# A three-stage kernel whose key and query loads, weight narrowing and dummy products are rearranged

## The chip, the cores and the metric

The program runs on one core of one Trainium2 chip. The metric is the device time of one launch, in microseconds (us). The kernel before was timed three times; each time also covers a little outside the profiled span.

## The reference

Three stages run one after the other. The first is a gated linear attention over 4 batches, 8 heads, 768 steps and head dimension 40, written as a recurrence over time:

```python
m_new = np.maximum(f_gate[:, :, t] + m, i_gate[:, :, t])
f_stab = np.exp(f_gate[:, :, t] + m - m_new)
i_stab = np.exp(i_gate[:, :, t] - m_new)
C = f_stab[:, :, None, None] * C + i_stab[:, :, None, None] * np.einsum('bhd,bhe->bhde', vt, kt)
n = f_stab[:, :, None] * n + i_stab[:, :, None] * kt
h_tilde = np.einsum('bhde,bhe->bhd', C, qt)
y[:, :, t] = sigmoid(o_gate[:, :, t]) * h_tilde / np.maximum(np.abs(np.einsum('bhd,bhd->bh', n, qt)[:, :, None]), 1.0)
```

The second is a soft mixture of experts over the 3072 tokens of width 320 (8 experts with 4 slots each, hidden width 1024, softmax over the tokens and over the slots). The third is an MLP, `relu(x @ w_in) ** 2 @ w_out`, with hidden width 2048.

## The kernel before

The 32 heads of all batches go in 11 groups of three (the last has two), and the 768 steps in 6 chunks of 128, so that the first stage is a loop over 66 units (group g, chunk c); unit i is 6g + c. The loop is software-pipelined: unit i issues the score products of unit i + 2 (`e_st`, L454), the decay exponentials of unit i + 3 (`e_exp`, L437, ScalarE), their mask (`e_sel`, L444, GpSimd), the product of both (`e_pm`, L466, VectorE), the state update (`e_u` L479, `e_uc` L498, `e_mask` L514), and for every second unit the products with v (`e_av`, L539), beside the product of q with the state (`e_inter`, L524). Between them a list of fillers is advanced: the gating of x, the expert logits of a batch that is done, and, as the last in rank, `win_all`.

`win_all` brings the weights w_in into a form that the third stage uses. They come in 10 windows of 128 x 1024 words (L163, 512 KB each) in two halves of the tile `stage`, and each window is narrowed to 128 x 512 by two ScalarE instructions (L140, L141) and two VectorE instructions (L143, L147). A filler stops at each `yield`; the letter says at which point of a unit it may go on ("W" once a unit, "A" for ScalarE, "n" for VectorE).

The program has its own order: no scheduler moves anything. All loads are issued by SyncE (SP) in the order of the program, and a request waits there until its buffer is free, with everything behind it. A group's k (three blocks of 40 x 768 words, 120 KB each, `load_kb`, L202) and q (120 x 768 words, 360 KB, `load_q`, L206) lie in one of two buffers, `par0` and `par1`, by the group's parity. The k of group g + 1 is requested at chunk 0 of group g, right before its q, and so into the buffer of group g - 1. Its k is last read by `e_st`, which runs two units ahead, and its q by `e_inter` of its last chunk. Other loads in the same queue are x (128 x 640, 320 KB, L221), v and k by tokens (369 and 360 KB, L215), the expert weights w1 (16 of 640 KB, L116) and w2 (16 of 640 KB, L123; the first two of them go into `stage` when `win_all` is done with it), and w_out (L962).

The start is a string, `START`, that is run token by token: `~30` stands for 30 dummy bf16 products on the identity matrix (`warm`, L192), `M2` for `e_mb` of chunk 2 (L423), `T0` for `e_st`, and `1f` and the like for steps of the gate preparation of chunks 0 and 1 (2: chunks 2 and 3; 3: chunks 4 and 5); `2q` are transposes (L331) and `2l` is a subtraction on VectorE (L351) that `M2` reads. After the 66 units come the rest of the experts (from 160 us on) and the third stage (from about 208 us on, L1283 to L1369).

Of the kernel before, what the change touches and what calls it, by code (L numbers as in the profile page):

```python
# [32 lines left out]
WO = (4, 5, 9)  # L33
START = "~30 1f 1i 1m 1h 1p 1b 1B 1aG 1r 2f 1u 1A 1v 1q 1l M0 2iG E0 M1 K0 W T0 T1 2m E1 K1 3f 2p 2b 2a ~14 2h 3i 3m 2B Z0 2r 2A 2v 2u P0 3p 3bG D0 3h Z1 ~3 2q 2l M2 E2 D0 P1 3a 3A 3B K2 D0 D0 3r 3u D0 | 3l 3v 3q | D1 D1 | D1 D1 D1 |"
REBIAS = 2.0**-112
# [7 lines left out]
def kernel(  # L43
# [16 lines left out]
    nc = tc.nc  # L60
# [73 lines left out]

    def narrow(dst, nt_, src, res=None):
        hi = src.rearrange("p (n w) -> p n w", w=2)[:, :, 1]
        low = src.bitcast(U16).rearrange("p (n w) -> p n w", w=4)[:, :, 1]
        di = dst.bitcast(I32)
        yield "A"
        nc.scalar.activation(dst, hi.bitcast(F32), AF.Copy, scale=REBIAS)  # L140
        nc.scalar.activation(nt_, low, AF.Copy, scale=2.0**-13, bias=2.0**-14 - 0.5)  # L141
        yield "n"
        nc.vector.scalar_tensor_tensor(  # L143
# [12 lines left out]
    def win_all():  # L156
# [13 lines left out]
        for n, (i, h) in enumerate(wins):  # L170
            yield "W"
            t2 = load(n + 1) if n + 1 < len(wins) else None
            yield from narrow(wi[:, i, NW * h : NW * h + NW], raw[:, 4 * NW : 5 * NW], t)
            t = t2
# [15 lines left out]
    def warm(n, t=None):  # L190
        for _ in range(n):
            nc.tensor.matmul(dum if t is None else t[:, 0:256], lhsT=zb[:, 0:128], rhs=zb, start=True, stop=True)  # L192

    kin, vin, xb = {}, {}, {}
    kbd = [par[i][0 : 3 * D, 0 : 3 * S].rearrange("p (j s) -> p j s", j=3) for i in range(2)]
# [8 lines left out]
    def load_q(g, cs=slice(0, S)):  # L204
        h0, nh = groups[g]
        nc.sync.dma_start(out=qin[g][0 : nh * D, cs], in_=q_t[h0 * D : (h0 + nh) * D, cs])  # L206

# [634 lines left out]
    def run(seq):  # L842
        for ch in seq.split():
            if ch[0] == "~":
                warm(int(ch[1:]))
            elif ch[0] in "MEKTP":
                {"M": e_mb, "E": e_exp, "K": e_sel, "T": e_st, "P": e_pm}[ch[0]](0, int(ch[1:]))
            elif ch[0] in "123":
                begin[ch[0]][ch[1]](*ch[2:])
            else:  # L850
                begin[ch[0]](*ch[1:])
# [10 lines left out]
    xq = [(b, c) for b in range(1, B) for c in range(0, NC, 2)]  # L862
    for i, (g, c) in enumerate(units):
        if c == 0 and g + 1 < NG:
            load_kb(g + 1)
            load_q(g + 1)
# [594 lines left out]
```

## Time and profile before

| | us |
|---|---|
| three runs | 410.29, 415.21, 408.58 |
| their median | 410.29 |
| the profiled execution, as timed | 411.04 |
| its span, from the first to the last instruction | 409.3 |
| mean granted clock of TensorE | 0.986 |
| TensorE (PE) busy | 383.4 |
| VectorE (DVE) busy | 263.7 |
| ScalarE (ACT) busy | 252.9 |
| GpSimd (POOL) busy | 101.5 |

All numbers of the rows below belong to the one profiled execution, whose time outside the span is 411.04 - 409.3 = 1.7 us. PEclk is the granted clock of TensorE as a share of 2.4 GHz; 0.50 is its lower level of 1.2 GHz. A matmul of fp32 data shows as two records.

### The profile page before, as it was taken

To read this page: it belongs to the slowest core of one execution; us is meant where nothing else is said; L and a number is where in the kernel's file an instruction comes from. 1 tells how busy PE (TensorE), PEld (TensorE's weight loads), DVE (VectorE), ACT (ScalarE), POOL (GpSimd) and SP (SyncE) were. 2 spreads that over 40 slices of the span, in tenths; PEclk is the share of its full clock that TensorE was granted. 3 is DMA by queue.
4 is the path that set the end of the run, shared out by engine and by line. 5 is a ranking of instruction groups with operands and counts; after the bars stand their busy time and mean duration, and the time that the engine had idled before them with its cause. 6 is when DMAs were issued, how large, how long until landed. Compare 5 with 4: busy or idle time off the path is not lost.

```text
span 409.3 us, 9150 instructions
## 1 busy us (share of the span) xinstructions
PE 383.4 (94%) x3435; PEld 337.0 (82%) x3435; DVE 263.7 (64%) x612; ACT 252.9 (62%) x575; POOL 101.5 (25%) x208
## 2 busy tenths in 40 slices
PE   6798987999699999999898999999999999999996
PEld 4697776888698887543377999999999999999996
DVE  8847787987457666545579965655655655655551
ACT  3678667657265654334479786667667667667662
POOL 5555555656654765500000000000000000000000
PEclk9799999999999999999999999999999999999999
DMA  7587569759975976879800001001001001001001
GB/s 200 169 319 245 197 208 348 217 160 346 281 246 186 285 218 254 262 260 360 339 1 2 0 16 50 2 0 66 2 1 66 1 2 64 2 0 66 2 2 64
DMA packets 18566, 56.37 MB, mean 138 GB/s; under 512 B 2346, under 2 KB 6154, under 8 KB 18138
## 3 DMA queue, kind: packets, MB, share of 16 engines
q1 hardware_dynamic: 18522, 55.79, 40.7%
q8 instruction: 27, 0.44, 0.4%
q14 instruction: 17, 0.14, 0.1%
HBM read 51.85 MB, written 3.93 MB: 136 GB/s over the span
## 4 chain that ended last, share of the span: by engine, by line
PE 69%; DMA 10%; DVE 6%; issue 4%; ACT 4%; POOL 4%; SPq 1%; DVEq 0%; POOLq 0%; ACTq 0%
PE ps_mb L1359 16%; PE ps_st L1359 15%; PE ps_lt L1359 8%; DMA par<-in_q_t_dram 7%; PE ps_st L454 6%; PE ps_o L1283 4%; DMA ring<-in_w_dram 3%; PE ps_o L539 3%; PE ps_o L524 3%; PE ps_st L479 2%; PE ps_m L1283 2%; PE ps_mb L423 2%; PE ps_m L654 1%; POOL cbd L514 1%; PE ps_st L1079 1%
## 5 line engine op out<-in xcount | busy, mean ns | idle before, releaser
L1306 DVE CAST hi<-ring 128x512 fp32r<-128x512 f32 x91 | 38.8, 426 | 60.8 <-ACT ring L1305 50.7
L437 ACT ACTIVATE w<-ps_mb,qt 128x128 f32<-128x128 f32 x192 | 56.6, 368 | 33.3 <-PE ps_mb L423 28.5
L1307 DVE TENSOR_TENSOR lo<-ring,hi 128x512 fp32r<-128x512 f32 x96 | 66.5, 692 | 10.0
L1288 ACT ACTIVATE ring<-ps_o 128x512 f32<-128x512 f32 x65 | 38.9, 599 | 36.6 <-PE ps_o L1283 36.6
L454 PE MATMUL ps_st<-par 120*128 120x128 f32 (+1 forms) x384 | 56.3, 284 | 3.9 <-DMA par<-in_q_t_dram 3.9
L1305 ACT ACTIVATE ring<-ring 128x512 f32<-128x512 f32 x91 | 57.5, 632 | 2.9
L454 PEld LDWEIGHTS ps_st<-par 120*128 120x128 f32 (+1 forms) x384 | 50.0, 198 | 4.9 <-issue 3.9
L1359 PE MATMUL ps_mb<-wohlh,hi 128*128 128x320 f32 x160 | 49.6, 311 | 0.0
L1359 PE MATMUL ps_mb<-wohlh,lo 128*128 128x320 f32 x160 | 49.5, 310 | 0.0
L1359 PE MATMUL ps_mb<-wohll,hi 128*128 128x320 f32 x160 | 49.3, 309 | 0.0
L1359 PE MATMUL ps_st<-wohlh,hi 128*128 128x320 f32 x144 | 44.8, 311 | 0.0
L1359 PE MATMUL ps_st<-wohlh,lo 128*128 128x320 f32 x144 | 44.7, 310 | 0.0
L1359 PE MATMUL ps_st<-wohll,hi 128*128 128x320 f32 x144 | 44.6, 310 | 0.0
L444 POOL TENSOR_SCALAR_AFFINE_SELECT w<-w 128x384 f32<-128x384 f32 (+1 forms) x66 | 35.2, 536 | 36.3 <-ACT w L437 33.1
L466 DVE TENSOR_TENSOR p<-ps_st,w 128x384 f32<-128x384 f32 (+1 forms) x66 | 35.5, 538 | 6.2 <-POOL w L444 3.8
L524 PE MATMUL ps_o<-cbd,par 120*128 120x123 f32 (+1 forms) x110 | 26.0, 318 | 7.9 <-POOL cbd L514 4.5
L1359 PEld LDWEIGHTS ps_mb<-wohll,hi 128*128 128x128 f32 x160 | 30.1, 188 | 1.3
L1288 ACT ACTIVATE ring<-ps_m 128x512 f32<-128x512 f32 x31 | 18.6, 599 | 18.8 <-PE ps_m L1283 18.8
L1359 PEld LDWEIGHTS ps_mb<-wohlh,hi 128*128 128x128 f32 x160 | 30.0, 188 | 0.0
L1359 PEld LDWEIGHTS ps_mb<-wohlh,lo 128*128 128x128 f32 x160 | 30.0, 188 | 0.0
L539 PE MATMUL ps_o<-par,p 128*64 128x41 f32 x768 | 29.1, 232 | 0.0
L1359 PEld LDWEIGHTS ps_st<-wohll,hi 128*128 128x128 f32 x144 | 27.1, 188 | 1.3
(267 smaller groups left out, 781.2 us busy)
## 6 DMA issues: line engine op xcount, KB each, us to landing
ring<-in_w_dram SPq DMA_DIRECT2D x24, 640.0 KB
stage<-in_w_in_dram SPq DMA_DIRECT2D x10, 512.0 KB
par<-in_w_dram SPq DMA_DIRECT2D x6, 640.0 KB
out_dram<-ring SPq DMA_DIRECT2D x24, 160.0 KB
par<-in_v_s_dram SPq DMA_DIRECT2D x10, 369.0 KB
par<-in_k_s_dram SPq DMA_DIRECT2D x10, 360.0 KB
par<-in_k_t_dram SPq DMA_DIRECT2D x29, 120.0 KB
par<-in_q_t_dram SPq DMA_DIRECT2D x9, 360.0 KB
```

What stands on the lines that cost most here:

```text
L437: nc.scalar.activation(w[:, j, :], mb[:, 128 * j : 128 * j + 128], AF.Exp, bias=qt3[:, c, h0 + j : h0 + j + 1])
L444: nc.gpsimd.affine_select(out=w, in_=w, pattern=[[0, nh], [1, 128]], compare_op=ALU.is_ge, fill=0.0, base=0, channel_multiplier=-1)
L454: nc.tensor.matmul(st[:, 128 * j : 128 * j + 128], lhsT=kbd[g % 2][0:nd, j, ts_], rhs=qin[g][0:nd, ts_], start=True, stop=True,)
L466: nc.vector.tensor_tensor(out=p, in0=sts.pop((g, c))[:, 0 : nh * 128].rearrange("p (n t) -> p n t", n=nh), in1=ws.pop((g, c)), op=ALU.mult,)
L524: nc.tensor.matmul(pos[g, c // 2][:, o0 : o0 + nv], lhsT=qin[g][0:nd, 128 * c : 128 * c + 128], rhs=cbds[g, c - 1][0:nd], start=True, stop ...
L539: nc.tensor.matmul(po[t0 : t0 + 64, o0 : o0 + DV], lhsT=p[:, j, t0 : t0 + 64], rhs=vin[g][:, c, j, :], start=True, stop=True,)
L1283: nc.tensor.matmul(t, lhsT=gst[n][:, 128 * k : 128 * k + 128], rhs=cst[tg], start=True, stop=True)
L1288: nc.scalar.activation(r, t, AF.Relu)
L1305: nc.scalar.activation(r, r, AF.Square)
L1306: nc.vector.tensor_copy(hi, r)
L1307: eng.tensor_tensor(out=lo, in0=r, in1=hi.bitcast(F32), op=ALU.subtract)
L1359: nc.tensor.matmul(acc[u][:, 0:DM], lhsT=l_[:, 128 * u : 128 * u + 128], rhs=wohl[r_, f // 8][:, f % 8, :], start=(f == 0 and a == 0), sto ...
```

## The change

Four things are changed at once. The two ScalarE instructions of a window are no longer issued one after the other: `narrow(..., apart=True)` stops after each of them until the next unit, so that a window takes at least three units and the ten windows stretch over more of the loop. `START` has 12 more dummy products in its first run of them and 10 more in its second, and a new kind, `~~5`, between `2q` and `M2`: 20 fp32 products, 10 of 128 columns and 10 of 41, each on 40 rows, alternately from row 0 and from row 64 and into two banks. The q of a group is requested as 128 rows; the last 8 belong to the next head and are not read. The k of group g + 2 is requested at chunk 4 of group g; that is two chunks before the place where it was requested (chunk 0 of group g + 1).

```diff
-START = "~30 1f 1i 1m 1h 1p 1b 1B 1aG 1r 2f 1u 1A 1v 1q 1l M0 2iG E0 M1 K0 W T0 T1 2m E1 K1 3f 2p 2b 2a ~14 2h 3i 3m 2B Z0 2r 2A 2v 2u P0 3p 3bG D0 3h Z1 ~3 2q 2l M2 E2 D0 P1 3a 3A 3B K2 D0 D0 3r 3u D0 | 3l 3v 3q | D1 D1 | D1 D1 D1 |"
+START = "~42 1f 1i 1m 1h 1p 1b 1B 1aG 1r 2f 1u 1A 1v 1q 1l M0 2iG E0 M1 K0 W T0 T1 2m E1 K1 3f 2p 2b 2a ~24 2h 3i 3m 2B Z0 2r 2A 2v 2u P0 3p 3bG D0 3h Z1 ~3 2q ~~5 2l M2 E2 D0 P1 3a 3A 3B K2 D0 D0 3r 3u D0 | 3l 3v 3q | D1 D1 | D1 D1 D1 |"
-    def narrow(dst, nt_, src, res=None):
+    def narrow(dst, nt_, src, res=None, apart=False):
...
         yield "A"
         nc.scalar.activation(dst, hi.bitcast(F32), AF.Copy, scale=REBIAS)
+        if apart:
+            yield "W"
+            yield "A"
         nc.scalar.activation(nt_, low, AF.Copy, scale=2.0**-13, bias=2.0**-14 - 0.5)
+        if apart:
+            yield "W"
         yield "n"
...
-            yield from narrow(wi[:, i, NW * h : NW * h + NW], raw[:, 4 * NW : 5 * NW], t)
+            yield from narrow(wi[:, i, NW * h : NW * h + NW], raw[:, 4 * NW : 5 * NW], t, apart=True)
...
+    def warm64(n):
+        t = bank("m")
+        for w in (128, 41):
+            for _ in range(n):
+                for o, r in ((dum, 0), (t, 64)):
+                    a = ident[r : r + 40]
+                    nc.tensor.matmul(o[:, 0:w], lhsT=a, rhs=a[:, 0:w], start=True, stop=True)
...
-        nc.sync.dma_start(out=qin[g][0 : nh * D, cs], in_=q_t[h0 * D : (h0 + nh) * D, cs])
+        n = 128 if (h0 + 3) * D + 8 <= q_t.shape[0] else nh * D
+        nc.sync.dma_start(out=par[g % 2][0:n, 3 * S : 4 * S][:, cs], in_=q_t[h0 * D : h0 * D + n, cs])
...
+        if c == NC - 2 and 0 < g + 2 < NG:
+            load_kb(g + 2)
+        if i == 0:
+            load_kb(1)
         if c == 0 and g + 1 < NG:
-            load_kb(g + 1)
             load_q(g + 1)
```

What this does to the order of instructions shows at three places. The first is SP's queue at units 0 to 5: k and q of group 2 go into par_70, x is the gate input of a later batch, and in_w_in are the windows. Before:

```order
L215 DMA par_71<-in_v_s_dram 128x738
L215 DMA par_71<-in_k_s_dram 128x720
L221 DMA x<-in_o_gate_dram 128x640 x3
L163 DMA stage<-in_w_in_dram 128x1024 x2
L202 DMA par_70<-in_k_t_dram 40x768 x3
L206 DMA par_70<-in_q_t_dram 120x768
```

And now (k is L215 there, v and k by tokens are L229, x is L235, the windows are L168, q is L220):

```order
L229 DMA par_71<-in_v_s_dram 128x738
L229 DMA par_71<-in_k_s_dram 128x720
L235 DMA x<-in_o_gate_dram 128x640 x2
L215 DMA par_70<-in_k_t_dram 40x768 x3
L235 DMA x<-in_o_gate_dram 128x640
L168 DMA stage<-in_w_in_dram 128x1024 x2
L220 DMA par_70<-in_q_t_dram 128x768
```

The k of group 2, which waits for its buffer, now stands ahead of the last x and of the first two windows.

The second place is SP's queue at units 28 to 36, from the k of group 6 (par_70) to the q of group 7 (par_71); in_w_dram into `ring` is w1, into `stage` w2. Before:

```order
L202 DMA par_70<-in_k_t_dram 40x768 x3
L206 DMA par_70<-in_q_t_dram 120x768
L221 DMA x<-in_o_gate_dram 128x640
L215 DMA par_70<-in_v_s_dram 128x738
L215 DMA par_70<-in_k_s_dram 128x720
L221 DMA x<-in_o_gate_dram 128x640
L123 DMA stage<-in_w_dram 128x1280
L116 DMA ring<-in_w_dram 128x1280
L123 DMA stage<-in_w_dram 128x1280
L116 DMA ring<-in_w_dram 128x1280
L202 DMA par_71<-in_k_t_dram 40x768 x3
L206 DMA par_71<-in_q_t_dram 120x768
```

Ahead of these stand an x (L221) and a w1 (L116). Now, from that x on, the k of group 6 standing ahead of it:

```order
L235 DMA x<-in_o_gate_dram 128x640
L116 DMA ring<-in_w_dram 128x1280
L220 DMA par_70<-in_q_t_dram 128x768
L235 DMA x<-in_o_gate_dram 128x640
L229 DMA par_70<-in_v_s_dram 128x738
L229 DMA par_70<-in_k_s_dram 128x720
L235 DMA x<-in_o_gate_dram 128x640
L168 DMA stage<-in_w_in_dram 128x1024
L116 DMA ring<-in_w_dram 128x1280
L215 DMA par_71<-in_k_t_dram 40x768 x3
L116 DMA ring<-in_w_dram 128x1280
L168 DMA stage<-in_w_in_dram 128x1024
```

The next row there is the q of group 7. Two windows of w_in stand where two loads of w2 stood; those two are now requested at units 59 and 60.

The third place is ScalarE at units 6 to 16, where L437 (now L451) are the exponentials, three a unit, and L140 and L141 (now L140 and L144) the two instructions of a window. Before:

```order
L140 ACTIVATE wi<-stage 128x512
L141 ACTIVATE stage<-stage 128x512
L437 ACTIVATE w<-ps_mb,qt_109 128x128 x9
L657 COPY xTw<-ps_m 120x512
L437 ACTIVATE w<-ps_mb,qt_109 128x128 x3
L657 COPY xTw<-ps_m 120x256
L140 ACTIVATE wi<-stage 128x512
L141 ACTIVATE stage<-stage 128x512
L437 ACTIVATE w<-ps_mb,qt_109 128x128 x3
L584 ACTIVATE rc<-num 128x18
L140 ACTIVATE wi<-stage 128x512
L141 ACTIVATE stage<-stage 128x512
```

Now:

```order
L140 ACTIVATE wi<-stage 128x512
L451 ACTIVATE w<-ps_mb,qt_109 128x128 x3
L144 ACTIVATE stage<-stage 128x512
L451 ACTIVATE w<-ps_mb,qt_109 128x128 x6
L671 COPY xTw<-ps_m 120x512
L451 ACTIVATE w<-ps_mb,qt_109 128x128 x3
L671 COPY xTw<-ps_m 120x256
L140 ACTIVATE wi<-stage 128x512
L451 ACTIVATE w<-ps_mb,qt_109 128x128 x3
L598 ACTIVATE rc<-num 128x18
L144 ACTIVATE stage<-stage 128x512
```

The VectorE pair of a window (L143 and L147) stands after units 5, 6, 11, 12, 13, 17, 18, 19, 23 and 30 before, and after units 7, 11, 17, 23, 30, 34, 40, 47, 52 and 58 now.

## Rows read from the trace of the kernel before

**Rows 1.** The page: busy time of the engines, and the chain that ended last by engine.

```profile
PE 383.4 (94%) x3435; PEld 337.0 (82%) x3435; DVE 263.7 (64%) x612; ACT 252.9 (62%) x575; POOL 101.5 (25%) x208
...
PE 69%; DMA 10%; DVE 6%; issue 4%; ACT 4%; POOL 4%; SPq 1%; DVEq 0%; POOLq 0%; ACTq 0%
```

**Rows 2.** Stretches: start:end length, busy by engine, clock, DMA share, GB/s.

```profile
10.00:20.00 10.00, 7.34 (x51) 6.41 (x51) 8.19 (x20) 6.68 (x22) 5.22 (x7) 0.77 0.53 170
20.00:30.00 10.00, 10.00 (x125) 9.24 (x124) 4.84 (x16) 7.28 (x24) 5.93 (x12) 0.89 0.94 332
30.00:80.00 50.00, 42.92 (x562) 38.39 (x559) 41.22 (x97) 35.03 (x101) 29.02 (x57) 1.00 0.73 246
80.00:90.00 10.00, 10.00 (x139) 8.61 (x137) 7.63 (x23) 6.71 (x23) 5.56 (x12) 1.00 0.42 142
110.00:120.00 10.00, 8.79 (x92) 7.87 (x94) 4.17 (x13) 4.03 (x13) 3.35 (x6) 0.83 0.71 239
160.00:164.00 4.00, 3.67 (x22) 2.23 (x21) 2.82 (x14) 1.47 (x6) 3.27 (x7) 1.00 0.12 44
186.00:200.00 14.00, 12.36 (x146) 4.78 (x146) 8.73 (x19) 6.45 (x11) 0.00 (x0) 1.00 1.01 403
```

**Rows 3.** Timeline of PE at the start: start, length, instruction, [idle before <-releaser].

```profile
11.23 2.02 PE L192 MATMUL ps_lt<-ident 128*128 128x256 bf16 x17
...
16.27 0.48 PE L423 MATMUL ps_mb<-M,sel 96*128 96x128 bf16 x3 [2.26 <-DVE M L351]
```

**Rows 4.** The chain of waits at units 0 to 3: start, length, what.

```profile
18.00 1.29 PE ps_st L454 x6
...
21.99 0.98 PE ps_o L539 x24
...
23.59 0.67 PE ps_st L454 x6
...
26.26 0.83 PE ps_o L539 x24
```

**Rows 5.** Groups by line: two of a window's four instructions, busy and mean ns.

```profile
L143 DVE SCALAR_TENSOR_TENSOR stage<-stage 128x512 int32<-128x512 int32 x10 | 7.4, 745 | 5.2 <-ACT stage L141 5.2
...
L140 ACT ACTIVATE wi<-stage 128x512 f32<-128x512 f32 x10 | 6.8, 683 | 0.1
```

**Rows 6.** Timeline of PE: `e_st` issued by units 12, 18, 48 and 54.

```profile
44.38 0.84 PE L454 MATMUL ps_st<-par 120*128 120x128 f32 x6
...
59.20 0.84 PE L454 MATMUL ps_st<-par 120*128 120x128 f32 x6
...
130.44 0.84 PE L454 MATMUL ps_st<-par 120*128 120x128 f32 x6
...
142.96 0.84 PE L454 MATMUL ps_st<-par 120*128 120x128 f32 x6
```

**Rows 7.** Timeline of DVE at unit 31: the first of the tenth window's pair.

```profile
89.98 1.26 DVE L143 SCALAR_TENSOR_TENSOR stage<-stage 128x512 int32<-128x512 int32 x1
```

**Rows 8.** Timeline of PE where it waited for q.

```profile
95.94 0.94 PE L454 MATMUL ps_st<-par 120*128 120x128 f32 x6 [0.20 <-DMA par<-in_q_t_dram]
...
111.21 1.62 PE L454 MATMUL ps_st<-par 120*128 120x128 f32 x6 [3.21 <-DMA par<-in_q_t_dram]
...
138.79 0.94 PE L454 MATMUL ps_st<-par 120*128 120x128 f32 x6 [0.46 <-DMA par<-in_q_t_dram]
```

**Rows 9.** The chain of waits: the longest piece, from request to landing.

```profile
99.87 11.20 DMA par<-in_q_t_dram
```

**Rows 10.** Timeline of SP: requests.

```profile
20.71 1.01 SPq L163 DMA_DIRECT2D stage<-in_w_in_dram  x2
25.68 1.08 SPq L202 DMA_DIRECT2D par<-in_k_t_dram  x3
...
84.69 0.33 SPq L221 DMA_DIRECT2D x<-in_o_gate_dram  x1
```

**Rows 11.** Timeline of ACT: the first window's first instruction.

```profile
30.48 0.69 ACT L140 ACTIVATE wi<-stage 128x512 f32<-128x512 f32 x1
```

More of the change, by code (lines that the diff above doesn't have):

```diff
@@ L843, in run @@
         for ch in seq.split():
-            if ch[0] == "~":
+            if ch[:2] == "~~":
+                warm64(int(ch[2:]))
+            elif ch[0] == "~":
                 warm(int(ch[1:]))
```

## The prediction

> **What bounds the kernel now.** I read the page's chain by engine first, then the clock by stretches, then PE's timeline where it is idle, and SP's requests behind those places. PE is busy 94% of the span and makes 69% of the chain [rows 1], so time is saved where PE is idle or slow, and only there. From about 208 us on nothing is touched by the change. The loop of 66 units before it has three kinds of loss. At the start the clock is below full: its mean is 0.77 between 10 and 20 us and 0.89 between 20 and 30 [rows 2]; since it has two levels, 1.2 and 2.4 GHz, that is 4.6 us and 2.2 us at the lower one. PE had waited 2.26 us for VectorE before `M2` at 16.27 [rows 3], and then worked without a gap, slowly: six score records take 1.29 us at 18.00 and 0.67 us at 23.59 [rows 4]. Between 30 and 80 us PE is busy 42.92 of 50 us [rows 2], 7.08 idle. Third, PE waits three times for a q, 3.21 us the longest [rows 8], and the clock is 0.83 in the stretch that this wait lies in, 110 to 120 us [rows 2]: 3.4 us at the lower level.
>
> **The dummy products.** The 12 in front end long before anything waits for them. The second batch had 17 in 2.02 us [rows 3], 0.119 us each; 10 more are 1.2 us, and it ends at 14.4 instead of 13.25. Behind it the transposes `2q` go on to about 14.8, and then come the 20 new fp32 products, which are 40 records. No row shows products on 40 rows, so I bound them: 20 records at 0.67 / 6 = 0.112 us and 20 at 0.83 / 24 = 0.035 us [rows 4] make 2.9 us if they run one after another, half of it if the two of a pair run side by side. They end at 17.7 or 16.3; `M2` could start at 16.27, so it is delayed by 1.4 us or not at all. Nothing covers that: PE's queue is the chain there. I take 0.7. The Trainium skill ("TensorEngine Tiling", section Key Properties) says that tiles on different rows work independently, in parallel; by it the delay is 0 and the sum 0.7 lower, and no row here shows it.
>
> In return the clock may stay up. From 16.27 to 21.99, where the chain leaves the slow stretch, are 5.72 us; at 0.67 / 1.29 of the time [rows 4] they are 2.97, a gain of 2.75 at most, and none if the clock falls all the same. ScalarE, busy 7.28 of 10 us from 20 to 30 [rows 2], does not become faster with PE and has the third preparation in its queue, so I take 1.5. **Start: -1.5 + 0.7 = -0.8** (ends: -2.75, and +1.4 if the clock falls anyway).
>
> **The first windows come later.** The k of group 2 now stands ahead of the third x and of windows 0 and 1. It was issued at 25.68, waiting for the last score product of group 0; the windows had gone out at 20.71 [rows 10]. Everything behind it waits too: the windows leave at about 25.68 + 1.08 + 0.35, less the 0.8 gained, 26.3 us. Ahead of window 0 are 360 and 320 KB; with its own 512 KB that is 1.22 MB, 3.7 us at the 332 GB/s of that stretch [rows 2], so it lands near 30 to 31 (an estimate, from these rows). Its first ScalarE instruction ran at 30.48 [rows 11] and would be due about 0.8 us earlier; exponentials queue behind it. Between 0 and 2 us; PE's three units of lead take most of it. **+0.5.**
>
> **The windows spread.** Before, nine of the ten pairs of VectorE instructions stand at units 5 to 23, now four do. One instruction is about 0.7 us [rows 5], so a window is 1.4 us on each of two engines, both of which also carry the exponentials, masks and state updates in order. What a window costs PE can be read off the groups: units 12 to 17, with three windows, take 59.20 - 44.38 = 14.82 us, units 48 to 53, with none, 142.96 - 130.44 = 12.52 [rows 6], so 0.77 a window. Five windows leave: 3.8 us. By the idle time it is 5/9 of 7.08 = 3.9. I take **-3.9**; the ends are 0 (something else would have been late at the same places) and the whole 7.08. The five land in the later groups. The nearest row says that this is free: the tenth window's pair, there already, ran at 89.98 [rows 7] and PE had no idle time between 80 and 90 [rows 2]. The other end is the same 0.77 each, 3.8. I lean on the nearer row: **+0.8.**
>
> **q and k.** A q of 128 rows is 384 KB instead of 360. It could gain at most 1/16 of the 11.20 us [rows 9], 0.7, if it ran on a sixteenth engine with fewer rows for each, and it could cost 24/360 of its own transfer, under 0.1. I take 0. The Trainium skill ("DMA: Bandwidth & Descriptors", section Why a DMA increments its semaphore by 16 and not by 1) lets a transfer use the largest number up to 16 that divides its rows: 15 engines for 120 rows, 16 for 128, 8 rows each both times; by it the gain is 0, and no row here tells the engines apart.
>
> The k sooner counts in the backlog that the late q meets. Since q may only go when its buffer is free (99.87), the time to landing, 11.20 us [rows 9], is what lies ahead of it. From the x at 84.69 [rows 10], where SP had been stopped, to that q's landing at 111.07 the requests come to 6329 KB in 26.4 us, 240 KB/us. Now the k of group 6 is ahead of that x, in a stretch with a DMA share of 0.42 [rows 2], two w2 are gone, and two windows come in: 6329 - 360 - 1280 + 1024 + 48 for two larger q = 5761 KB, which is 568 KB or 2.4 us less. The wait of 3.21 becomes 0.8. The three stretches below 1.00 make 4.6 + 2.2 + 3.4 = 10.2 us at the lower level, and the mean of 0.986 over 409.3 us is 11.5, so the waits of 0.20 and 0.46 [rows 8] brought next to no fall, and I expect none behind 0.8: in those 3.4 us at the lower level half the time is lost, 1.7 us. With 0.3 of the two short waits that is -4.4. But the two windows that follow are 512 KB each in groups whose DMA is nearly full, and 0.9 us may come back there. **-3.5** (ends: 0, and -5.6 when all three waits and the slow stretch go).
>
> The two w2 now requested at units 59 and 60 have the time from 160 to 164 us, DMA share 0.12 [rows 2], as cover: 1280 KB at the 403 GB/s of a full stretch [rows 2] are 3.3 us. Without that cover they would push the last loads, which hold PE between 186 and 200 us, by as much. 0.
>
> **The sum**: -0.8 + 0.5 - 3.9 + 0.8 - 3.5 = -6.9; 411.04 - 6.9 = 404.1 us. The profiled execution lies 0.75 above the median of the three runs, 410.29, so I forecast **404.0 us**. Two per cent, about what a measurement of this kernel can tell from no change, are 8.2 us: 402.1 and 418.5.
>
> **The rivals.** *All of it works* (0.20): the pairs of dummies overlap, the clock stays up, no q is waited for, window 0 is in time: -2.75 - 3.9 + 0 - 5.6 = -12.2, 398.8 us (397 to 401.5). For it: every loss has its own remedy. Against it: ScalarE at the start, and transfers that are tight.
>
> *The transfers become the bound* (0.20): four windows, 2 MB, go from before 84 us to behind it, where the loads were already waited for. Then a q is waited for as long as before, the clock falls once, and -3.5 goes: 407.6 us (406 to 410). For it, the share of 1.0 in busy stretches; against it, 0.42 and less in others.
>
> *ScalarE and VectorE become the bound in the later groups* (0.07), the case on the slower side: five windows, each 2 x 0.683 + 2 x 0.745 = 2.86 us [rows 5] that PE waits in full, 14.3 instead of 0.8: 417.6 us (411 to 418.6). It decides from the point where these engines have less than 1.4 us idle per unit on the way of an exponential or a state update; the free pair at 89.98 [rows 7] speaks against it.
>
> *It does not do what it says* (0.05): the clock falls as before, and the idle time only changes its place, since the pace between 30 and 80 us is set by the chain of small instructions itself: 409 to 411.
>
> **Chances.** The forecast, 401 to 407, has 0.48. The range 399.0 to 410.5 leaves out half of the first rival, nearly all of the slower one and a little of the last, 0.18 together. Faster by over 2%: 0.19 of the first rival and 0.07 of the forecast's lower edge, 0.26. Slower by over 2%: 0.02. Within: 0.72.
>
> **What would show it.** Clock 1.00 from 10 to 30 us, with `M2` no later than 17; PE idle under 4 us between 30 and 80, and units 12 to 17 near 13.3 us; the wait before `e_st` of unit 40 under 1 us and no stretch below 1.00 behind it; the loop's end some 7 us sooner, and the last loads before 200 us sooner by as much. I am wrong if the clock falls at the start behind the dummies, if PE is idle in units 30 to 60 behind a window, or if q is still waited for by 3 us.

## The result, and the profile after

| | before | after |
|---|---|---|
| median of four runs, us | 410.26 (408.58 to 415.21) | 396.39 (395.41 to 396.71) |
| the profiled execution, us | 411.04 | 396.40 |
| its span, us | 409.3 | 394.7 |
| mean granted clock of TensorE | 0.986 | 0.999 |

The ratio is 0.9671, with a 95% interval of 0.9636 to 0.9706: faster, and below the forecast range of 399.0 to 410.5. Ratios here leave out runs more than 1.5% above the fastest of their kernel (of the four before, 415.21), medians do not. The profiled executions differ by 14.64 us, and that is the sum explained here. The page of the changed kernel, engines and chain, against [rows 1]:

```profile
PE 381.7 (97%) x3497; PEld 337.2 (85%) x3497; DVE 264.8 (67%) x612; ACT 251.9 (64%) x575; POOL 103.3 (26%) x208
...
PE 79%; DMA 5%; ACT 3%; POOL 2%; DVE 2%; issue 2%; SPq 0%; DVEq 0%; ACTq 0%; POOLq 0%
```

The work of the other engines is the same. PE idles 13 us in the span where it idled 26, and makes 79% of the chain. The same stretches as in [rows 2] say where (start:end length, busy by engine, clock, DMA share, GB/s):

```profile
10.00:20.00 10.00, 9.64 (x106) 8.83 (x106) 8.67 (x21) 6.85 (x23) 5.13 (x7) 1.00 0.48 165
20.00:30.00 10.00, 9.53 (x136) 8.71 (x135) 5.26 (x16) 7.58 (x24) 6.35 (x13) 1.00 0.84 269
30.00:80.00 50.00, 48.48 (x641) 43.33 (x640) 39.53 (x101) 33.61 (x105) 33.94 (x65) 1.00 0.73 240
110.00:120.00 10.00, 10.00 (x126) 8.21 (x125) 8.73 (x24) 5.77 (x20) 5.68 (x11) 1.00 0.76 273
```

The clock is 1.00 in all of them. Between 30 and 80 us PE is idle for 1.52 us instead of 7.08, and it waits for no q. A ledger can be kept on a row that both kernels have once a unit, `e_st` (L454 before, now L468). Those issued by unit 2 (at 23.43 us before), then by units 12, 18, 48 and 54 [rows 6], now begin so:

```profile
22.45 0.83 PE L468 MATMUL ps_st<-par 120*128 120x128 f32 x6
...
42.76 0.84 PE L468 MATMUL ps_st<-par 120*128 120x128 f32 x6
...
54.76 0.84 PE L468 MATMUL ps_st<-par 120*128 120x128 f32 x6
...
117.75 0.84 PE L468 MATMUL ps_st<-par 120*128 120x128 f32 x6
...
129.55 0.61 PE L468 MATMUL ps_st<-par 120*128 120x128 f32 x4
```

The group of units 12 to 17 takes 54.76 - 42.76 = 12.00 us where it took 14.82, the one of units 48 to 53 11.80 where it took 12.52. Read over all units, the ledger is this (us):

```
                                               after - before   this step
e_st at 23.43 before (the start)                    -0.98         -0.98
e_st at 73.85 (units 6 to 23, the windows)          -7.25         -6.27
e_st at 105.55 (the short wait for q, unit 34)      -7.72         -0.47
e_st at 116.89 (the long wait, slow clock)         -12.69         -4.97
e_st at 163.55 (the third wait; end of the loop)   -13.41         -0.72
end                                                -14.64         -1.23
```

### The profile page after: what moved, and what is told of

Same layout as the page of the kernel before. It is cut to its first block, busy times and chain, and to the rows that moved or that the text cites. A ratio compares the mean times of both kernels' runs of the same rounds, so it can differ in the third digit from the quotient of the medians.

```text
span 394.7 us, 9282 instructions
## 1 busy us (share of the span) xinstructions
PE 381.7 (97%) x3497; PEld 337.2 (85%) x3497; DVE 264.8 (67%) x612; ACT 251.9 (64%) x575; POOL 103.3 (26%) x208
## 4 chain that ended last, share of the span: by engine, by line
PE 79%; DMA 5%; ACT 3%; POOL 2%; DVE 2%; issue 2%; SPq 0%; DVEq 0%; ACTq 0%; POOLq 0%
PE ps_mb L1378 17%; PE ps_st L1378 15%; PE ps_lt L1378 8%; PE ps_st L468 8%; PE ps_o L553 5%; PE ps_o L538 4%; PE ps_o L1302 4%; DMA ring<-in_w_dram 3%; PE ps_st L493 3%; PE ps_mb L437 2%; PE ps_m L668 2%; PE ps_m L1302 2%; PE ps_lt L674 2%; DMA stage<-in_w_in_dram 1%; PE ps_st L1098 1%
## 5 line engine op out<-in xcount | busy, mean ns | idle before, releaser
L451 ACT ACTIVATE w<-ps_mb,qt 128x128 f32<-128x128 f32 x192 | 56.7, 370 | 22.9 <-PE ps_mb L437 18.7
L468 PE MATMUL ps_st<-par 120*128 120x128 f32 (+1 forms) x384 | 54.0, 276 | 0.0
L468 PEld LDWEIGHTS ps_st<-par 120*128 120x128 f32 (+1 forms) x384 | 47.9, 191 | 0.5 <-issue 0.5
L458 POOL TENSOR_SCALAR_AFFINE_SELECT w<-w 128x384 f32<-128x384 f32 (+1 forms) x66 | 36.8, 559 | 37.4 <-ACT w L451 28.7
L1302 PE MATMUL ps_o<-cst,gst 128*128 128x512 f32 x65 | 26.2, 403 | 2.0 <-ACT gst L1345 2.0
```

Of the source, the lines that this page charges most:

```text
L451: nc.scalar.activation(w[:, j, :], mb[:, 128 * j : 128 * j + 128], AF.Exp, bias=qt3[:, c, h0 + j : h0 + j + 1])
L458: nc.gpsimd.affine_select(out=w, in_=w, pattern=[[0, nh], [1, 128]], compare_op=ALU.is_ge, fill=0.0, base=0, channel_multiplier=-1)
L468: nc.tensor.matmul(st[:, 128 * j : 128 * j + 128], lhsT=kbd[g % 2][0:nd, j, ts_], rhs=qin[g][0:nd, ts_], start=True, stop=True,)
L1302: nc.tensor.matmul(t, lhsT=gst[n][:, 128 * k : 128 * k + 128], rhs=cst[tg], start=True, stop=True)
```

## The experiments

**One part at a time.** Each of the four parts alone, on the kernel before. Their diffs are the four pieces of the change's diff: START with `warm64`; `apart`; the k requests; the q request.

> The kernel before with only the new start (12 and 10 more dummy products and the 20 pairs on 40 rows). Start theory: the clock stays at 1.00 from 10 to 30 us although M2 starts half a microsecond later (16.8), e_st of unit 3 runs at 22.45 instead of 23.43, and nothing behind it takes that back: 410.3 - 1.0 = 409.3 us. Rival (the clock held only because other work had moved as well): the clock falls again behind 16.8 and the start costs +0.5. Rival (the gain is lost at the next stall, because the windows' stalls are set by ScalarE and VectorE and not by PE): e_st of unit 12 at 41.2 as before, 410.3.

> The kernel before with only the windows narrowed apart. Theory of the prediction (a window costs about 0.77 us wherever it stands, less of them early is the gain): -3.9 + 0.8, some 407 us, with stalls of 0.5 to 1.1 us left behind each window. Theory formed from the changed kernel's trace (what costs is that the four instructions stand in one unit, so that VectorE waits for ScalarE with the state update queued behind it): all 6.3 us between units 9 and 24 go, no stall behind any window, some 404 us. On the q of group 7: two windows come in where two loads of 640 KB stood, 256 KB less ahead of it, about 1.1 us: a wait of 2.1 us is left; if the wait is gone here already, the k sooner is not what removed it.

> The kernel before with only the k of a group requested two chunks sooner. Theory of the prediction (the backlog ahead of q counts): 360 KB less ahead of the q of group 7, 1.5 us of its wait of 3.21, so 1.7 us of waiting stay and the clock may fall behind it: -1.5 to -3.2, 407 to 409 us, with +0.5 at the start where the first windows come later. Rival (it is the k sooner that frees the queue): all three waits and the slow clock go, -6.1, 404 us. Rival (it needs the spread windows as well): wait of 3 us as before, 410 us.

> The kernel before with only the q requested as 128 rows instead of 120. Theory of the prediction: 0, 410.3 us, the three waits for q unchanged within 0.2 us. Rival (128 rows spread better over the engines that move them): the time from request to landing of the q of group 7 falls from 11.2 us by 0.7 or more, and the wait of 3.21 us and the clock behind it with it, down to 406 us.

| part alone | median, us | ratio to before on that chip (409.73 us) |
|---|---|---|
| new start | 409.36 | 0.9953 (0.9899 to 1.0007) |
| windows apart | 398.67 | 0.9759 (0.9677 to 0.9842) |
| k sooner | 412.36 | 1.0033 (0.9975 to 1.0091) |
| q as 128 rows | 405.63 | 0.9924 (0.9879 to 0.9968) |

The product of the four ratios is 0.967, that of the whole change. The windows carry most; q, put at 0, is the second; the k, on which -3.5 rested, shows no gain alone. With the windows apart alone, `e_st` at 73.85 comes 9.30 us sooner, 1.54 of them by the start, where this execution's clock was at half between 10 and 13 us and full from 14 us on, without the new dummies: 7.76 us for the windows, so all of the 7.08 idle and more. The wait for the q of group 7 shrinks to 0.82 us there. With the q alone all three waits for q are gone and the windows' stalls stay (before `e_inter` 5.2 us for the state and 3.2 for VectorE). The kernel with the k alone lost too much clock in its profiled execution (mean 0.967) for a sure reading of single stalls; in it PE waits 1.67 us for the q of group 7, about what the prediction's theory left of the 3.21, and for no other q.

These runs also show how unsteady the kernel before is: in 25 executions its mean clock lay between 0.974 and 0.992 and its time between 406.23 and 414.56 us. In the four of the changed kernel they lie between 0.999 and 1.000, and 395.41 and 396.71.

**One part taken back.** The whole change, without the k sooner; with q as 120 rows; with the old START.

```diff
-        if c == NC - 2 and 0 < g + 2 < NG:
-            load_kb(g + 2)
-        if i == 0:
-            load_kb(1)
         if c == 0 and g + 1 < NG:
+            load_kb(g + 1)
             load_q(g + 1)
```

> The whole change without the k sooner (k of group g + 1 at chunk 0 of g again). Theory A (the 128 rows of q, and the two loads of w2 that left, are what removed the waits for q; the k sooner is worth nothing): 396.4 us within 1, no wait for q over 0.5 us, the clock 1.00; the stalls at units 6 to 8 (0.80 and 0.45 us with the k sooner) a little shorter, since the first windows are not kept waiting. Theory B, the prediction's (the backlog ahead of q decides): 360 KB more ahead of the q of group 7, a wait of some 2 us and a slow stretch behind it, 399 to 400 us.

> The whole change with q requested as 120 rows again. Theory A (the rows of q decide how the transfers run; with 120 the loads around it are slow): waits for q return, 0.8 us at unit 40 and 0.5 us at unit 52 as in the kernel with the spread windows alone, clock falls in some of the runs, 397.5 to 400 us. Theory B, the prediction's (q as 128 rows is worth 0): 396.4 us within 0.7 and no wait for q over 0.2 us.

> The whole change with the old START (fewer dummy products, no pairs on 40 rows). Theory A (the dummies make sure that the clock stays up at the start, which without them it does in some runs and not in others): times from 395.8, where the clock stays up (e_st of unit 3 at 21.9), to 398 or 399 where it falls between 8 and 24 us; median 397.5. Theory B (the start never mattered, later stalls take it back): 396.4 in all runs, whatever the clock at the start.

| | median, us | ratio to before (409.14 us) |
|---|---|---|
| without the k sooner | 395.88 (395.08 to 396.23) | 0.9670 (0.963 to 0.971) |
| q as 120 rows | 398.32 (396.17 to 400.69) | 0.9714 (0.9661 to 0.9768) |
| old START | 397.17 (395.47 to 401.29) | 0.9719 (0.9649 to 0.9788) |

Without the k sooner nothing is lost, and no q is waited for: theory A. With 128 rows the k sooner is not needed. What the k does is seen at the first windows. In the changed kernel the chain of waits runs through the load of window 0, which was requested behind that k:

```profile
26.23 5.72 DMA stage<-in_w_in_dram
...
32.55 0.87 ACT w L451 x3
```

ScalarE in the changed kernel, and then in the kernel without the k sooner:

```profile
31.97 0.69 ACT L140 ACTIVATE wi<-stage 128x512 f32<-128x512 f32 x1 [2.36 <-DMA stage<-in_w_in_dram]
32.55 0.87 ACT L451 ACTIVATE w<-ps_mb,qt 128x128 f32<-128x128 f32 x3
```

```profile
29.49 0.69 ACT L140 ACTIVATE wi<-stage 128x512 f32<-128x512 f32 x1
31.03 0.88 ACT L451 ACTIVATE w<-ps_mb,qt 128x128 f32<-128x128 f32 x3 [0.84 <-PE ps_mb L437]
```

ScalarE, in order, holds an exponential behind the window's first instruction: that instruction runs at 31.97 in the changed kernel and the exponential at 32.55, and in the kernel without the k sooner at 29.49 and 31.03. `e_st` comes 1.51 us sooner from unit 11 on. The kernel without the k sooner gives 1.14 us of it back at 128 us, where `e_inter` waits 1.07 us for the state.

With 120 rows of q, theory A expected waits for q; the profiled execution has none, and lost its time (4.45 us by the ledger, all before 45 us) at a clock that fell between 16 and 24 and between 36 and 48 us, in spite of the new start. So with the windows apart and the k sooner q is in time either way. With 120 rows and the k at its old place PE waits 2.35 us for the q of group 7 (below), so that the k sooner takes that wait away as the prediction had it; the 128 rows take it away too, and either is enough for that, as far as one profiled execution of each shows. The medians of the two kernels with 120 rows, 398.32 and 398.59 on two chips, show no gain from it. The old START has a wider spread than expected, 395.47 to 401.29 us, with a mean clock from 0.987 to 0.996. Its profiled execution was at half clock between 10 and 14 us and still ended at a span of 393.8, sooner than the changed kernel's: `e_st` issued by unit 2 begins at 21.91 there against 22.45, so that a fall before `M2`, for which PE waits 1.21 us for VectorE, cost nothing that can be seen.

**The order inside a window.** In the whole change, all four instructions of a window in one unit again, with a unit's pause between windows; then ScalarE's two in one unit and VectorE's a unit later. Both have the windows at the same units within one, six pairs of VectorE by unit 23 where the spread kernel has four, so the two differ in the order and not in the pace. The diff of the first:

```diff
-            yield from narrow(wi[:, i, NW * h : NW * h + NW], raw[:, 4 * NW : 5 * NW], t, apart=True)
+            yield "A"
+            yield "W"
+            yield from narrow(wi[:, i, NW * h : NW * h + NW], raw[:, 4 * NW : 5 * NW], t)
```

> The whole change, but each window's two ScalarE and two VectorE instructions stand in one unit again, with a unit between windows so that their pace is about the spread one's (VectorE pairs behind units 5, 10, 12, 16, 18, 22, 29, 33, 39, 46 or one later). Theory of the prediction (the number of windows in the early groups is what counts; a window costs 0.77 us there and next to nothing later): five or six windows in units 5 to 24 cost as much as the spread ones, 396.4 to 398 us. Theory from the traces (VectorE, in order, waits for ScalarE's two instructions with the state update behind it, wherever the window stands): each of the ten windows stalls PE by 0.5 to 1.5 us, e_inter waits for the mask and for the state, some 6 us in all, and the clock falls behind the longest: 402 to 406 us.

> The whole change, but ScalarE's two instructions of a window stand together in one unit and VectorE's two a unit later, at the same units as in the kernel where all four stand together (399.0 us of span, PE waiting 1.91 us before e_inter at unit 8). Theory A (what costs is that VectorE waits in its queue for ScalarE, with the state update behind it): a unit's distance takes that wait away, the pair on ScalarE alone costs nothing, 396.4 us within 1. Theory B (the pair on ScalarE is too long ahead of the exponentials, the mask and the product follow late): the same stalls as with all four together, 400 to 401 us. Theory C (the number of windows per group, three to four more before unit 30 than in the spread kernel, is what costs): between, 398 to 399 us, with a stall behind the windows that stand two units apart.

Together: 401.17 us, ratio 0.979 (0.9741 to 0.984), 4.8 us slower than spread and just under what the theory from the traces expected. In pairs: 399.62, ratio 0.9723 (0.9663 to 0.9784), with clock falls in the profiled execution at the start and at 36 to 44 us; behind unit 12 the pairs cost 0.13 us against the spread kernel, where the four together cost 1.50. By the ledger that is theory A for the later windows, though the median is above its 396.4; of the first ones these two said little, since window 0 is late there and the clock falls behind it. So the four together were run again with the first window in time (below, "a better version", is the kernel that it is compared with).

> The kernel with all changes and the k of group 2 requested late (394.79 us), but each window's four instructions in one unit, two units apart at the closest. It takes the late first window out of the comparison made before (401.17 us with all four together in the whole change, 3.4 us of them at units 7 to 12). Theory A (VectorE waits for ScalarE with the state update behind it, at every window of the early groups): 1 to 2 us at the first three windows, 1.5 us at those of units 16 to 24, 397.5 to 399 us, with clock falls in some of the runs. Theory C (the late first window was what cost there, and the pace is what counts): 395 to 396 us, no stall over 0.5 us before unit 16.

It took 399.07 us (397.98 to 399.75, ratio 0.979, on another chip than the kernel that it is compared with), theory A. Here are its ScalarE, VectorE, GpSimd and PE at units 7 and 8 (start, length, instruction, [idle before <-releaser]):

```profile
33.36 0.68 ACT L140 ACTIVATE wi<-stage 128x512 f32<-128x512 f32 x1
33.93 0.67 ACT L144 ACTIVATE stage<-stage 128x512 int32<-128x512 uint16 x1
```

```profile
34.63 0.69 DVE L148 SCALAR_TENSOR_TENSOR stage<-stage 128x512 int32<-128x512 int32 x1 [1.76 <-ACT stage L144]
35.36 0.69 DVE L152 SCALAR_TENSOR_TENSOR wi<-wi,stage 128x512 int32<-128x512 int32 x1
35.97 0.33 DVE L514 SCALAR_TENSOR_TENSOR cu<-cbd,dec,ps_st 120x123 f32<-120x123 f32 x1
...
36.69 0.40 DVE L581 TENSOR_TENSOR num<-ps_o,tmp 128x246 f32<-128x246 f32 x1
```

```profile
36.38 0.39 POOL L530 TENSOR_TENSOR cbd<-cu,hm 120x123 f32<-120x123 f32 x1 [2.16 <-DVE cu L514]
```

```profile
37.24 0.46 PE L540 MATMUL ps_o<-cbd,par 120*128 120x123 f32 x2 [1.90 <-DVE num L581]
```

VectorE stood idle for 1.76 us with the window's instruction at the head of its queue, until ScalarE had done both of its own; the state update (L514) was behind it and GpSimd's mask waited for that. PE's row names L581, which stood in VectorE's queue behind the state update and ended last, 0.3 us after the mask. What VectorE idled before L148 behind ScalarE in the whole execution, first in the changed kernel and then with all four together in it (before: 5.2 us [rows 5]):

```profile
L148 DVE SCALAR_TENSOR_TENSOR stage<-stage 128x512 int32<-128x512 int32 x10 | 7.7, 774 | 0.0
```

```profile
L148 DVE SCALAR_TENSOR_TENSOR stage<-stage 128x512 int32<-128x512 int32 x10 | 7.5, 750 | 4.6 <-ACT stage L144 4.6
```

The ledger of this run against the same kernel with the windows apart: 2.08 us at this place (0.37 of them won back by unit 12), 0.78 at unit 17 and 0.84 at units 22 to 24, 3.33 us so far and no clock fall among them (another 0.94 is a fall at 18 to 24 us). A last step of 0.58 at unit 45 was not traced to a cause. The pace differs here too, six pairs by unit 23 against four.

**Why 128 rows.** First on the kernel before, with each q in two pieces, 112 and 8 rows or 60 and 60:

```diff
-        nc.sync.dma_start(out=qin[g][0 : nh * D, cs], in_=q_t[h0 * D : (h0 + nh) * D, cs])
+        n = (nh * D - 1) // 16 * 16
+        for r, e in ((0, n), (n, nh * D)):
+            nc.sync.dma_start(out=qin[g][r:e, cs], in_=q_t[h0 * D + r : h0 * D + e, cs])
```

> The kernel before with each q requested in two pieces, 112 rows and 8 rows: the same bytes as before. Theory A (120 rows leave one of the engines that move data without a part, and that is what slows the transfers around it; 112 rows give each the same): the waits for q at units 34, 40 and 52 go as with 128 rows, q of group 7 lands in 6 to 7.5 us instead of 11.2, and the time comes to 405 or 406 us. Theory B (only the request of all 128 rows does it, or the rows have nothing to do with it): a wait of 2.5 to 4 us at unit 40 as before, 409 to 410 us.

> The kernel before with each q requested in two pieces of 60 rows: as many requests as in the kernel with 112 and 8 rows, and the same bytes. Theory A (the split over the engines decides): nothing is won, a wait for q of 2.5 to 4 us at unit 40, 409 to 410 us, while 112 and 8 rows win 3 us or more. Theory B (what decides is the number of requests or where they fall in the eight that may be under way): the same as with 112 and 8 rows, whichever that is.

Ratios 0.9931 (0.9889 to 0.9974) and 0.9962 (0.9916 to 1.0009), and at unit 40 waits of 2.77 and 3.03 us: against theory A, but with the clock of the kernel before (0.975 and 0.974) in the way. So the four requests were compared in a kernel with next to no clock falls: new start, windows apart, k at its old place.

> The new start and the spread windows, with the k at its old place and q requested as 120 rows: the kernel to compare the next three with, in which hardly a clock fall disturbs. Theory A (120 rows are what makes q late): waits for q of 0.8 us at unit 40 and 0.5 us at unit 52, as in the kernel with the spread windows alone; about 397.5 us. Theory B (q's rows are worth nothing, as the prediction had it): the same as with 128 rows, no wait for q, 396 us.

> The same kernel with q requested as 128 rows (the whole change without the k sooner, timed once before at 395.88 us). Theory A: no wait for q, the slowest q lands 7 us after its request instead of 8.5, 1 to 2 us faster than with 120 rows, 396 us. Theory B: the same as with 120 rows within 0.7 us.

> The same kernel with q requested in two pieces of 112 and 8 rows. Theory A1 (an engine without a part is what makes q late): as with 128 rows, no wait for q, 396 us. Theory A2 (the even 8 rows for every engine, or the whole tile, is what counts) and theory C (a second request takes one of the places of what may be under way): waits for q as with 120 rows or longer, 397.5 to 398.5 us.

> The same kernel with q requested in two pieces of 60 rows, the control for the one with 112 and 8. Theory A1: waits for q as with 120 rows, 0.8 and 0.5 us, 397.5 us, more than a microsecond slower than with 112 and 8 rows. Theory C (the number of requests decides): the same as with 112 and 8 rows.

> The kernel with the new start, the spread windows and the k at its old place, with q requested as 128 rows in two pieces of 64. Theory even share (what counts is that every engine gets as many rows as the others; 112 and 8 rows leave eight engines with one row more): no wait for q, as with 128 rows in one request, 396.5 us. Theory of the single request (a second request is as bad as the uneven share): a wait of 1.5 us or more at unit 40 as with the other two-piece kernels, 398 to 399 us.

| q requested as | four runs: median, us | ratio to before on that chip | wait for q at unit 40 | at unit 52 | q of group 7, request to last mark |
|---|---|---|---|---|---|
| 120 rows | 398.59 (397.47 to 400.53) | 0.9717 | 2.35 | none | 9.48 |
| 128 rows | 396.51 (395.69 to 397.14) | 0.9666 | none | none | 5.74 |
| 112 and 8 | 398.11 (396.99 to 401.16) | 0.9712 | 1.76 | none | 8.63 and 8.47 |
| 60 and 60 | 398.88 (396.48 to 399.98) | 0.9711 | 1.57 | 0.79 | 7.67 and 8.28 |
| 64 and 64 | 400.14 (397.51 to 403.96) | 0.9818 | 1.64 | none | 7.84 and 8.20 |

The last row is from another chip than the four above it. The times set 128 rows apart from 120 only; 112 and 8 and 60 and 60 overlap with both, the intervals of all the ratios overlap, and it is the waits, in one profiled execution each, that tell the splits from the single request. The last column is read from the marks of landing that a trace has for each request.

The q of group 7 was requested at 91.67 and 92.62 us with 120 and 128 rows. Three stretches of each kernel (120 rows, then 128):

```profile
92.00:98.00 6.00, 6.00 (x91) 5.30 (x89) 4.03 (x13) 4.63 (x16) 4.42 (x9) 1.00 0.99 276
96.00:102.00 6.00, 3.65 (x50) 3.29 (x49) 3.73 (x12) 1.92 (x7) 3.11 (x8) 1.00 1.03 286
102.00:106.00 4.00, 4.00 (x42) 3.69 (x41) 3.41 (x7) 2.35 (x7) 2.10 (x4) 0.57 0.58 192
```

```profile
92.00:98.00 6.00, 6.00 (x74) 5.29 (x73) 4.04 (x11) 4.88 (x15) 4.14 (x9) 1.00 0.93 284
96.00:102.00 6.00, 6.00 (x76) 5.80 (x74) 4.70 (x14) 3.72 (x12) 4.78 (x10) 1.00 1.00 379
102.00:106.00 4.00, 4.00 (x56) 3.32 (x54) 3.96 (x9) 2.74 (x9) 1.38 (x4) 1.00 0.46 141
```

From 96 to 102 us the rates differ, 286 and 379 GB/s, but not for the same loads: with 128 rows the q had landed by 98.36 and the loads behind it were moving. From 92 to 98 us, when both kernels had k and q under way, the rates are 276 and 284 GB/s, and from the request of q to its last mark 282 and 300: 6% apart, where the times are 9.48 and 5.74 us. The rate alone does not make this q late. The chain and PE of the kernel with 120 rows:

```profile
91.67 9.48 DMA par<-in_q_t_dram
```

```profile
101.19 0.94 PE L467 MATMUL ps_st<-par 120*128 120x128 f32 x6 [2.35 <-DMA par<-in_q_t_dram]
```

What differs more is how far apart the parts of q land: leaving out a first mark at 0.50 us with 120 rows (on which more below), the marks run from 3.67 to 9.48 us after the request with 120 rows and from 3.96 to 5.74 with 128. The third of the three k loads ahead of it, the same 40 rows in both, took 8.29 and 5.39. Two more pairs of executions differ in the rows of q alone, and there the steps are not all as large: on the kernel before the q took 11.20 us with 120 rows and 6.36 with 128, that k 11.07 and 9.88; in the whole change (k sooner) the q took 7.47 and 6.36, the k 6.90 and 6.51. So the rows of q are a cause of its lateness, with the same sign in all three pairs; the mechanism is open. A part that is left out with 120 rows is not enough for it: the 112 rows have no such early mark, and PE still waits 1.76 us. An equal share for all is not enough either: 64 and 64 rows wait 1.64. Only the single request of 128 rows was in time, in all three executions that had it with the k at its old place. (The profile puts the wait of 1.57 us down to issue, at the same `e_st`; the last mark of the second piece comes at 100.34 us, just before that `e_st` at 100.43.)

**A better version.** The whole change with the k of group 2 alone at its old place, behind the first windows.

```diff
-        if c == NC - 2 and 0 < g + 2 < NG:
+        if c == NC - 2 and 0 < g < NG - 2:
             load_kb(g + 2)
-        if i == 0:
-            load_kb(1)
+        if i in (0, NC):
+            load_kb(1 + g)
```

> The whole change, except that the k of group 2 alone is requested where it was before, behind the third x and the first two windows; the k of groups 3 to 10 stays two chunks sooner. Theory A (in the changed kernel the first window is late because it waits behind that k, and an exponential waits behind it on ScalarE: 1.5 us at units 6 to 9; the stall of 1.07 us at 128 us, which the kernel without any k sooner has, is avoided by the later k): both are won, e_st of unit 10 at 38.3 instead of 39.8, span 393.2, time 394.9 us. Rival (the time won at the start is waited for again by the loads behind, q or the last weights): 396 us, with a wait for a load that the changed kernel does not have.

394.79 us (394.67 to 395.12), ratio to before on that chip 0.9603 (0.956 to 0.9646), span 393.4, clock 1.000. The ledger stands 1.51 us ahead of the changed kernel's from unit 11 to the end of the loop, and between 30 and 80 us PE is busy 49.72 of 50 us. All four of its runs are below all four of the changed kernel (395.41 to 396.71, timed at another time); the intervals of the two ratios still overlap, so that it is the faster one rests on the ledger of one execution each as much as on the times.

## Why the prediction was wrong

The direction and every place were right, the size was half: -6.9 forecast, -14.64 measured. (By its own terms the forecast for the median should have been 410.29 - 6.9 = 403.4 and not 404.0; that slip is not what failed.) By its terms:

- **Start**, -0.8: the ledger has -0.98. The price came out near as well, in part by luck: `M2` starts 0.52 us later, where 0.7 was taken as the middle between 0 and 1.4. The timeline of PE, the second run of dummies, the first pairs, the last ones and `M2`:

```profile
11.22 3.11 PE L197 MATMUL ps_lt<-ident 128*128 128x256 bf16 x27
...
14.43 0.37 PE L205 MATMUL ps_lt<-ident 40*128 40x128 f32 x1
14.44 0.37 PE L205 MATMUL ps_m<-ident 40*128 40x128 f32 x1
14.64 0.27 PE L205 MATMUL ps_lt<-ident 40*128 40x128 f32 x1
14.65 0.27 PE L205 MATMUL ps_m<-ident 40*128 40x128 f32 x1
14.76 0.27 PE L205 MATMUL ps_lt<-ident 40*128 40x128 f32 x1
...
16.46 0.28 PE L205 MATMUL ps_lt<-ident 40*128 40x41 f32 x1
...
16.57 0.28 PE L205 MATMUL ps_lt<-ident 40*128 40x41 f32 x1
16.58 0.28 PE L205 MATMUL ps_m<-ident 40*128 40x41 f32 x1
16.79 0.34 PE L437 MATMUL ps_mb<-M,sel 96*128 96x128 bf16 x3
```

  The two of a pair start 0.01 us apart: they do run side by side, as the Trainium skill has it for tiles on different rows ("TensorEngine Tiling (Array Packing)", Key Properties). The 0.035 us for a record of 41 columns did not carry over: the pairs settle at 0.11 us apart at 41 columns as at 128, so that the delay is not the 0 that side by side alone would give: the overlap makes them cheaper than the upper bound, the 41 columns dearer than the lower, and the middle came out near. But that the clock stays up is no sure effect: in the profiled executions it fell somewhere between 9 and 28 us in all seven with the old START and in four of the thirteen with the new one. The start alone, 0.9953 with an interval up to 1.0007, is not shown to be faster.
- **The first windows come later**, +0.5 between 0 and 2: 1.51 us, by both kernels that ask for the k of group 2 late. The cause and the landing (31.95 us by the chain, 30 to 31 forecast) were right, but the step "PE's three units of lead take most of it" failed: the exponentials wait in ScalarE's queue.
- **The windows spread**, -3.9 and +0.8 for the five that land later: -6.27, or -7.78 without the late first window. Here it failed most. The price of 0.77 was read off a group with three windows and taken for the price of a window wherever it stands. It was the price of the order: four instructions in one unit, VectorE waiting for ScalarE with the state update behind. The group of units 12 to 17 still has windows and takes 12.00 us, less than the 12.52 that stood for one with none; that 12.52 was no clean base either, since it holds the wait of 0.46 us for q at 138.79 [rows 8]. Taken apart, a window costs nothing that the ledger shows. The 0.8 for the five that land later was not paid.
- **q and k**, -3.5: -6.16 (0.47 + 4.97 + 0.72). The step "I take 0" for the 128 rows failed: alone, they remove all three waits and their slow clock. The k sooner, from which -3.5 was worked out, has no wait for q left to remove where q has 128 rows. The backlog was not wrong as a cause where q has 120: there the k sooner leaves no wait of the 2.35 us. But the bytes ahead of q were not the only thing that sets when it lands: the rows of the request move its last mark by 1.1 to 4.8 us. The bound of "at most 1/16" was worked out from a count of engines and from no row. The rule that the Trainium skill gives ("DMA: Bandwidth & Descriptors", section Why a DMA increments its semaphore by 16 and not by 1) agrees with the marks: with 120 rows one mark comes 0.50 us after the request, 3.17 us ahead of all others, with 128 rows none before 3.96. The conclusion that the gain is then 0, since each engine has 8 rows either way, is what the runs refute. The 0.9 for the windows that follow was not lost either.
- **The rest**, 0: -1.23 behind the loop. The w2 moved to units 59 and 60 did find cover, and the last loads even came sooner against the work: PE waits for them 0.81 us there instead of 1.41. That the whole 1.23 is theirs was not tried apart.

Of the rivals, "all of it works" was nearest, 398.8, with 0.20; it still carried -3.9 for the windows, though the whole 7.08 idle was listed as an end of that term. With all the ends as listed, -2.75 - 7.08 - 5.6, the sum would have been 395.6; the range stopped at 399.0. "Transfers become the bound" and "ScalarE and VectorE become the bound" did not happen: the later groups have the windows and no wait behind one.

## What to carry to other kernels

When an engine works in order, look at what stands behind an instruction that waits for another engine: here four dependent instructions of a filler in different units instead of one were worth 1.1% to 1.2% (399.07 to 394.79, 401.17 to 396.39 us; the two of a pair were timed apart, and the pace is somewhat slower too) and 2.4% on the kernel before, without one of them removed. A request's cost is not its bytes alone: where a load is late, look at how far apart its parts land, and try the full 128 rows in one request. A rate over a fixed stretch says little where the two kernels move different loads in it. And when the parts of a change each have an end, let the range reach the sum of the ends on the side where the parts don't exclude each other.

## What the runs showed of the hardware

- The same q landed later as 120 rows than as 128, from request to last mark: 11.20 us against 6.36 on the kernel before, 9.48 against 5.74 with the new start and the windows apart, 7.47 against 6.36 in the whole change. In two requests, however split, the slower piece took 8.20 to 8.63 us where the single one of 128 rows took 5.74. Why is open.
- The clock falls are not the same from one execution to the next: the kernel before was at mean clocks of 0.974 to 0.992 on one chip, with 8 us between its fastest and its slowest execution. The changed kernel, whose PE idles 1.54 us between 30 and 140 us, stayed at 0.999 or more. The Trainium skill ("TensorE: Matmul & The Clock Gate", section Part 1: The HAM clock gate) calls the warm-up run-variable for one and the same kernel; here it is the falls later on that vary from one execution to the next.
- fp32 products on 40 rows at partitions 0 and 64, into two banks, start 0.01 us apart, and pairs settle at 0.11 us apart at 41 columns as at 128.
